# One weight decode, one token-sum step, one passage decode and two low halves moved in an attention, GLU and MLP kernel

## The chip, the cores and the metric

The kernel runs on one core of a Trainium2 chip. The time is microseconds on the device from the start of the launch to its end; the median of several runs is compared. Everything here is float32 work: each product of two float32 matrices is made of three TensorE passes over a high and a low part, high by high, high by low and low by high.

## The reference

```python
x = attn_out.transpose(0, 2, 1, 3).reshape(2304, 512)   # linear attention over 4 x 8 heads, 576 tokens
xn = x / sqrt(mean(x * x) + 1e-6) * rms_g
x = (silu(xn @ w_gate) * (xn @ w_val)) @ w_out           # 512 -> 1536 -> 512
h = x @ w2_in                                            # 512 -> 2048
out = (h * sigmoid(h)) @ w2_out                          # 2048 -> 512
```

The weights come as 64-bit floats. The kernel loads them as pairs of 32-bit words and turns them into float32 by itself.

## The kernel before

The tokens stand in five blocks: blocks 0 to 3 have 512 tokens, block 4 has 256. `xs[j]` holds a block's input as a high and a low part. The 12 GLU slices (128 columns of `w_gate` and `w_val`, 128 rows of `w_out`) and 16 MLP slices are worked through in turn, all blocks for a slice before the next. Slices 0 and 1 and slice 2 (`sweeps`) are done with plain three-pass products, 12 matmuls of 128x128 by 128x512 for a block. From slice 3 on (`groups`, nine of the GLU and eight pairs of the MLP) `quad` computes two blocks at once from sums of weights and sums of tokens, so that seven half products do the work of eight.

**Decoding weights.** A slice is loaded by a DMA on SP's queue into one of two buffers, raw0 or raw1. `w_decode` (`dec`) takes five steps on VectorE (L146 to L157) and two adds on GpSimd (L160); after them the raw buffer is free for the next load. Then ScalarE makes the high part (`hi`, with four scalings at L168 for gate and value, and L486) and VectorE the low one (`lo`, L490). `sum12` and `sum34` (GpSimd, L376) and `shi`, `slo` make the sums of weights. `WeightQueue.plan` lists these jobs for each group; an entry that is only `(0,)` does nothing. `tick` runs the next entry. In `stream` the products yield their planned TensorE time, and the driving loop at the end of the kernel runs a tick when enough of it has gone by, unless `quiet`, `calm` or `hold` is set; `quad` sets `hold` and calls `tick` at places written out by hand.

**Token sums.** `token_sums` returns a list of steps: sums and differences on VectorE (L407, L410), `tok_high` on ScalarE (L399) and `tok_low` on VectorE (L402). The loop pops one after each `wq.rest` of planned time. For the second pair of blocks `tok_high(2)` writes into `ya[1]`.

**The order at the first `quad`.** In `stream`, `order` goes through (3, f0), (4, f0), (1, slice 2), (0, slice 2), (3, slice 2), (2, slice 2), (4, slice 2). The output products (`g2_glu`, L281) of one entry are emitted inside the value product of the next (`mixed` in `g1_glu`). For blocks 1 and 0 the outputs are copied by ScalarE (L293) to stages, which GpSimd adds into DRAM with accumulating DMAs (L297, two for a block); block 1's stages are the halves of `ya[1]`. Every block's `h` is split into a high part (ScalarE, L198) and a low one (VectorE, L199) behind the gate-value product (L242). At the entry (0, slice 2), `wq.tick()` runs the first entry of the queue:

```python
(0, lambda: dec(a0, 0), lambda: load(u, bs[0], 0)),
```

that is, the decode of group 0's gate weights from raw0 and the load of its `w_out` slice into raw0. The last step of group 0's token sums issues the load of the value weights into raw1, on the same queue.

**The passage from GLU to MLP.** Group 9 (`std`) is the first MLP group. Its decodes run in the last GLU group's second `quad`, whose ticks stand after each half product. There, block 3's last outputs are added (L303), made into a high part by ScalarE (L305) and a low part by VectorE (`low`, L271). `plus` (L658) adds `e` to a product in PSUM, which frees that bank for the next product.

Of the kernel before, what the change touches and what calls it, by code (L numbers as in the profile page):

```python
# [20 lines left out]
def kernel(  # L21
# [22 lines left out]
    KC = DM // P  # L44
# [14 lines left out]
    NB, NE = len(blocks), 3  # L59
# [162 lines left out]
    def g1_glu(f, j, hs, mid):  # L222
        wq.need((1, "g", f))
        p = ps_tile("ps_g" if blocks[j] == TB * P else "ps_y", [P, blocks[j]])
        yield from proj2(wt[1, "g", f], j, p)
        s = pools["s"][0].tile([P, blocks[j]], F32, tag="s", name="s", bufs=pools["s"][1])
        nc.scalar.activation(out=s, in_=p, func=AF.Silu)
        mixed = f == sweeps[1][1][0] and blocks[j] == TB * P
        if blocks[j] == TB * P and not mixed:
            yield from mid  # L230
        wq.need((1, "v", f))
        p = ps_tile("ps_g" if blocks[j] == TB * P else "ps_y", [P, blocks[j]])
        last = proj2(wt[1, "v", f], j, p)
        if mixed:
            yield next(last)
            step = next(last)
            yield from mid
            wq.calm, wq.quiet = True, False
            yield step
        yield from last  # L240
        wq.calm = False
        nc.vector.tensor_tensor(out=s, in0=s, in1=p, op=ALU.mult)  # L242
        if mid is None:
            wait.append(lambda: hs.update({f: split_h(s, j)}))
            return
        hs[f] = split_h(s, j)
        if blocks[j] < TB * P:
            yield from mid
# [15 lines left out]
    def g2_glu(fs, j, hs, first, last, calm=False):  # L264
        wq.need(*[(1, "o", f) for f in fs])
        staged = j < NE and not last
        y = ya[j].rearrange("p (c t) -> p c t", c=KC)
        nn = 3 * len(fs)

        def low(d):  # L270
            (nc.gpsimd if 0 < j < NE else nc.vector).tensor_tensor(  # L271
                out=xs[j][:, 1, d, :], in0=y[:, d, :],
                in1=xs[j][:, 0, d, :].bitcast(F32), op=ALU.subtract,
            )

        for d in range(KC):
            ps = ps_tile("ps_y", [P, blocks[j]])
            n = 0
            for f in fs:
                for a, c in PASS:  # L280
                    nc.tensor.matmul(  # L281
                        out=ps,
                        lhsT=wt[1, "o", f][:, a, d * P:(d + 1) * P],
                        rhs=hs[f][:, c, :],
                        start=(n == 0),
                        stop=(n == nn - 1),
                    )
                    n += 1
            if staged:
                if d % 2 == 0:  # L290
                    o = stage()
                if d % 2 == 0 or calm:
                    nc.scalar.activation(out=o[:, d % 2, :], in_=ps, func=AF.Copy)  # L293
                else:
                    nc.vector.tensor_copy(out=o[:, 1, :], in_=ps)
                if d % 2:
                    nc.gpsimd.dma_start(  # L297
                        out=kept(j, d // 2), in_=o.rearrange("p t d -> p (t d)"), accum_op=ALU.add
                    )
            elif first:  # L300
                nc.scalar.activation(out=y[:, d, :], in_=ps, func=AF.Copy)
            else:
                nc.vector.tensor_tensor(out=y[:, d, :], in0=ps, in1=y[:, d, :], op=ALU.add)  # L303
            if last:
                nc.scalar.activation(out=xs[j][:, 0, d, :], in_=y[:, d, :], func=AF.Copy)  # L305
                if d:
                    low(d - 1)
                if d == KC - 1:
                    low(d)
            yield nn * blocks[j] / 2365  # L310

# [47 lines left out]
            yield 0.216 * nn  # L359

    KH = KC // 2
    tok, sums, ready, wait, owed, stages = {}, [], set(), [], [], []

    def stage():
        stages.append(stages.pop(0))
# [3 lines left out]
    std = next(u for u, g in enumerate(groups) if g[0] == 2)  # L369
# [13 lines left out]
    def token_sums(p, temp, end, early=False, eng=nc.vector):  # L383
        half = lambda j, a, h: xs[2 * p + j][:, a, KH * h:KH * (h + 1), :].bitcast(F32)
        u = {}

        def tok_high(n, x):
            if n == 1:
                tok[p, n] = [xs[2 * p + 1][:, a, :KH, :] for a in range(2)]
            elif p:  # L390
                tag = f"ya{(1, 0, 2)[n - 2]}"
                v = big.tile([P, KC * TB * P], F32R, tag=tag, name=tag)
                v = v.rearrange("p (a c t) -> p a c t", a=2, c=KH)
                tok[p, n] = [v[:, a] for a in range(2)]
            else:
                tok[p, n] = [
                    w_tile(1, 3 + 2 * (n - 2) + a).rearrange("p (c t) -> p c t", c=KH) for a in range(2)
                ]
            nc.scalar.activation(out=tok[p, n][0], in_=x, func=AF.Copy)  # L399

        def tok_low(n, x):
            nc.vector.tensor_tensor(out=tok[p, n][1], in0=x, in1=tok[p, n][0].bitcast(F32), op=ALU.subtract)  # L402
            ready.add((p, n))

        def whole(k, j, h):
            u[k] = u[1] if k == 3 and p == 0 else temp(k).rearrange("p (c t) -> p c t", c=KH)
            nc.vector.tensor_tensor(out=u[k], in0=half(j, 0, h), in1=half(j, 1, h), op=ALU.add)  # L407

        def minus(out, x, y):
            eng.tensor_tensor(out=out, in0=x, in1=y, op=ALU.subtract)  # L410

        ready.difference_update([(p, n) for n in range(1, 5)])
        return [
            lambda: whole(1, 1, 0),
            lambda: whole(0, 0, 0),
            lambda: minus(u[0], u[1], u[0]),
            lambda: whole(2, 1, 1),
            lambda: minus(u[1], u[2], u[1]),
            lambda: minus(u[2], u[2], u[0]),
            lambda: tok_high(3, u[1]),  # L420
            *([
                lambda: tok_low(3, u[1]),
                lambda: whole(3, 0, 1),
                lambda: minus(u[3], u[3], u[2]),
                lambda: tok_high(2, u[2]),
                lambda: tok_low(2, u[2]),
            ] if early else [
                lambda: (tok_low(3, u[1]), tok_high(2, u[2])),
                lambda: tok_low(2, u[2]),
                lambda: whole(3, 0, 1),  # L430
                lambda: minus(u[3], u[3], u[2]),
                lambda: None,
            ]),
            lambda: tok_high(4, u[3]),
            lambda: (tok_low(4, u[3]), end(0)),
        ], [
            lambda: tok_high(1, u[0]),
            lambda: (tok_low(1, u[0]), end(1)),
        ]

    class WeightQueue:
# [12 lines left out]
        def load(self, u, key, n):  # L454
            if u >= len(groups):
                return
            key = self.keys(u)[0][key] if isinstance(key, int) else key
            kind, nm, f = key
            src = {"g": w_gate, "v": w_val, "o": w_out, "i": w2_in, "p": w2_out}[nm]
            self.st[key] = State()  # L460
            w_load((0, 0, key, wrows(src, f) if nm in "op" else wcols(src, f)), self.st[key], n)
# [9 lines left out]
        def plan(self, u):  # L471
# [8 lines left out]
            def dec(key, n):  # L480
                for k in range(7):
                    w_decode((0, 0, key, None), st[key], k, n)
# [14 lines left out]
            def lo(key):  # L497
                split_lo(mf(key), st[key].t)
                wt[key] = st[key].t
# [55 lines left out]
            elif std <= u < std + NSTD:  # L555
# [9 lines left out]
                    (1, lambda: lo(a1), lambda: hi(a0), lambda: dec(bs[1], 1), lambda: load(u + 1, 1, 1))  # L565
                    if u == std else (1, lambda: hi(a0)),
                    (0, lambda: lo(a0)),
                    (0, lambda: dec(bs[0], 0), lambda: load(u + 1, 0, 0)),
                    *[(0,)] * (1 + (u == std)),
                    (1, lambda: hi(bs[1])),  # L570
                    (0, lambda: lo(bs[1])),
                    (0,),
# [47 lines left out]
    wq = WeightQueue()  # L620
# [11 lines left out]
    def quad(u, ys, hs, p=0, skip=0, done=True):  # L632
# [19 lines left out]
        def silu(x, tl):  # L652
            nc.scalar.activation(out=tl, in_=x, func=AF.Silu)  # L653
            return tl
# [59 lines left out]
            wq.release(("s", u, 1))  # L714
        t12 = plus(pc)
        silu(t12, t12)

        def last_half():
            if kind == 1:
# [95 lines left out]
    def stream():  # L815
# [28 lines left out]
        for n, (j, fs) in enumerate(order):  # L844
            hs, mine = {}, n == len(order) - 1
            wq.quiet = n == 3
            if n == 3:
                wq.tick()
            for f in fs:
                yield from g1_glu(f, j, hs, None if mine else pend)  # L850
                pend = pend if mine else ()
# [19 lines left out]
        for u, (kind, fs) in enumerate(groups):  # L871
# [6 lines left out]
            if std <= u < std + NSTD:  # L878
# [3 lines left out]
                    stages[:] = [ya[3][:, n * 1024:][:, :1024] for n in range(2)] + [ya[4]]  # L882
                while wait:
                    wait.pop(0)()
                each = [(2, 2)] * 4 if first else [(2, 2), (1, 1), (0, 0), (0, 0)]
                for n, k in enumerate(each):
                    if n == 2 and not first:
# [5 lines left out]
                    j = 3 - n // 2 if first else 1 - n // 2  # L893
# [767 lines left out]
    with tc.manual_schedule():  # L1661
# [50 lines left out]
        n = 0  # L1712
# [59 lines left out]
```

## Time and profile before

| | |
|---|---|
| median of 3 runs | 944.88 us (944.24 to 945.15) |
| the profiled execution | 945.14 us, of which the span of instructions is 943.3 us |
| TensorE matmul busy | 926.8 us (98% of the span) |
| VectorE, ScalarE, GpSimd busy | 703.9, 531.0, 476.2 us (75%, 56%, 50%) |
| mean granted TensorE clock | 0.994 |

PE is TensorE's matmuls, PEld its weight loads, DVE VectorE, ACT ScalarE, POOL GpSimd, SPq the queue of the sync engine, which issues DMAs. Busy time is the time in which an instruction of that engine runs. A line number is that of the kernel before.

### The profile page before, as it was taken

To read this page: it belongs to the slowest core of one execution; us is meant where nothing else is said; L and a number is where in the kernel's file an instruction comes from. 1 tells how busy PE (TensorE), PEld (TensorE's weight loads), DVE (VectorE), ACT (ScalarE), POOL (GpSimd) and SP (SyncE) were. 2 spreads that over 40 slices of the span, in tenths; PEclk is the share of its full clock that TensorE was granted. 3 is DMA by queue.
4 is the path that set the end of the run, shared out by engine and by line. 5 is a ranking of instruction groups with operands and counts; after the bars stand their busy time and mean duration, and the time that the engine had idled before them with its cause. 6 is when DMAs were issued, how large, how long until landed. Compare 5 with 4: busy or idle time off the path is not lost.

```text
span 943.3 us, 17366 instructions
## 1 busy us (share of the span) xinstructions
PE 926.8 (98%) x6480; PEld 777.2 (82%) x6480; DVE 703.9 (75%) x1323; ACT 531.0 (56%) x1157; POOL 476.2 (50%) x495
## 2 busy tenths in 40 slices
PE   8999999997999999999999989999999999999998
PEld 6888878885888888888888878888888888888886
DVE  6998999866787877877787888877674757575633
ACT  5999977644455455455545455656545454545442
POOL 8888755105445545445454644376554545453411
PEclk9999999999999999999999999999999999999999
DMA  7645543304648648658657742546878787878677
GB/s 188 170 126 149 145 131 97 151 23 92 133 89 174 139 97 184 142 101 170 153 99 151 177 158 68 183 109 133 158 129 165 136 159 143 153 150 148 113 148 165
DMA packets 98788, 129.65 MB, mean 137 GB/s; under 512 B 29456, under 2 KB 75792, under 8 KB 98704
## 3 DMA queue, kind: packets, MB, share of 16 engines
q0 software_dynamic: 17280, 59.78, 36.4%
q1 hardware_dynamic: 81152, 68.70, 25.4%
q8 instruction: 51, 0.84, 0.4%
q14 instruction: 33, 0.27, 0.1%
q10 hardware_dynamic: 272, 0.07, 0.0%
HBM read 54.59 MB, written 69.21 MB: 131 GB/s over the span
## 4 chain that ended last, share of the span: by engine, by line
PE 91%; DMA 3%; DVE 2%; POOL 2%; ACT 1%; issue 1%; SPq 0%; DVEq 0%; POOLq 0%; ACTq 0%
PE g L626 29%; PE y L333 21%; PE y L281 13%; PE g L205 7%; PE y L205 6%; PE b L1238 3%; PE b L205 3%; PE kv L1318 2%; PE b L1422 2%; PE b L1211 2%; PE b L1638 2%; POOL m L160 1%; DMA out_dram<-ya 1%; PE b L1518 1%; PE b L1398 1%; DMA raw<-in_moe_w_out_dram 1%
## 5 line engine op out<-in xcount | busy, mean ns | idle before, releaser
L160 POOL TENSOR_TENSOR m<-m,raw 128x512 int32<-128x512 int32 x136 | 202.5, 1490 | 208.2 <-DVE m L157 114.1
L333 PE MATMUL y<-w,h 128*128 128x512 f32 (+1 forms) x870 | 211.9, 388 | 0.2 <-ACT h L198 0.2
L333 PEld LDWEIGHTS y<-w,h 128*128 128x128 f32 x870 | 162.0, 188 | 34.0 <-ACT h L198 0.7
L626 PE MATMUL g<-xs,w 128*128 128x512 f32 x720 | 181.7, 390 | 0.0
L626 PEld LDWEIGHTS g<-xs,w 128*128 128x128 f32 x720 | 134.2, 188 | 27.3
L281 PE MATMUL y<-h,w 128*128 128x512 f32 (+1 forms) x648 | 150.6, 370 | 5.9 <-ACT h L198 5.9
L199 DVE TENSOR_TENSOR h<-s,h 128x512 fp32r<-128x512 f32 (+1 forms) x117 | 88.0, 764 | 89.2 <-ACT h L198 89.1
L281 PEld LDWEIGHTS y<-h,w 128*128 128x128 f32 x648 | 115.5, 191 | 28.2 <-ACT h L198 6.3
L358 POOL DMA_DIRECT2D out_dram<-ya x64 | 59.0, 987 | 117.1 <-DVE ya L352 49.4
L198 ACT ACTIVATE h<-s 128x512 fp32r<-128x512 f32 (+1 forms) x117 | 69.0, 594 | 37.5 <-DVE s L242 15.1
L350 ACT ACTIVATE ya<-y 128x512 f32<-128x512 f32 x82 | 48.9, 596 | 71.3 <-PE y L333 67.3
L297 POOL DMA_DIRECT2D out_dram<-w x52 | 46.0, 889 | 71.5 <-ACT w L293 67.0
L205 PE MATMUL g<-xs,w 128*128 128x512 f32 x336 | 80.3, 390 | 0.0
L1287 ACT ACTIVATE e<-b,nb 128x128 f32<-128x128 f32 x272 | 76.1, 425 | 7.4 <-issue 4.0
L352 DVE COPY ya<-y 128x512 f32<-128x512 f32 x52 | 35.8, 688 | 59.3 <-PE y L333 59.3
L638 ACT ACTIVATE g<-g 128x512 f32<-128x512 f32 x60 | 34.9, 581 | 70.2 <-PE g L626 69.6
L205 PEld LDWEIGHTS g<-xs,w 128*128 128x128 f32 x336 | 62.7, 188 | 12.8
L626 PE MATMUL g<-w,w 128*128 128x512 f32 x270 | 69.7, 394 | 2.7 <-DVE s L658 2.7
L490 DVE TENSOR_TENSOR w<-m,w 128x512 fp32r<-128x512 f32 x74 | 70.3, 950 | 0.2 <-ACT w L486 0.2
L653 ACT ACTIVATE s<-s 128x512 f32<-128x512 f32 x42 | 26.6, 633 | 76.5 <-DVE s L658 76.5
L626 PE MATMUL g<-ya,w 128*128 128x512 f32 x270 | 68.5, 389 | 0.0
L205 PEld LDWEIGHTS y<-xs,w 128*128 128x128 f32 x480 | 61.1, 190 | 2.1
(142 smaller groups left out, 1593.5 us busy)
## 6 DMA issues: line engine op xcount, KB each, us to landing
out_dram<-ya POOLq DMA_DIRECT2D x54, 512.0 KB, 6.9
out_dram<-w POOLq DMA_DIRECT2D x54, 512.0 KB, 7.3
raw<-in_moe_w_out_dram SPq DMA_DIRECT2D x28, 512.0 KB, 4.7
raw<-in_moe_w_in_dram SPq DMA_DIRECT2D x16, 512.0 KB, 4.6
out_dram<-ya SPq DMA_DIRECT2D x14, 512.0 KB, 4.0
raw<-in_moe_w_gate_dram SPq DMA_DIRECT2D x12, 512.0 KB, 4.1
raw<-in_moe_w_val_dram SPq DMA_DIRECT2D x12, 512.0 KB, 4.8
qT<-e SPq DMA_DIRECT2D x72, 64.0 KB, 2.3
```

Of the source, the lines that this page charges most:

```text
L160: tt(out=mi, in0=mi, in1=(low if step == 5 else high).bitcast(I32), op=ALU.add)
L198: nc.scalar.activation(out=ht[:, 0, :], in_=s, func=AF.Copy)
L199: nc.vector.tensor_tensor(out=ht[:, 1, :], in0=s, in1=ht[:, 0, :].bitcast(F32), op=ALU.subtract)
L205: nc.tensor.matmul(out=ps, lhsT=w[:, a, cc * P:(cc + 1) * P], rhs=xs[j][:, c, cc, :], start=(n == 0), stop=(n == 3 * KC - 1),)
L281: nc.tensor.matmul(out=ps, lhsT=wt[1, "o", f][:, a, d * P:(d + 1) * P], rhs=hs[f][:, c, :], start=(n == 0), stop=(n == nn - 1),)
L297: nc.gpsimd.dma_start(out=kept(j, d // 2), in_=o.rearrange("p t d -> p (t d)"), accum_op=ALU.add)
L333: nc.tensor.matmul(out=ps, lhsT=hs[f][:, a, t * P:(t + 1) * P], rhs=wt[2, "p", f][:, c, d0:d1], start=(n == 0), stop=(n == nn - 1),)
L350: nc.scalar.activation(out=o[:, t % 2, :], in_=ps, func=AF.Copy)
L358: nc.gpsimd.dma_start(out=rows, in_=o[p0:p1], accum_op=ALU.add)
L490: eng.tensor_tensor(out=v[:, 1, :], in0=x, in1=v[:, 0, :].bitcast(F32), op=ALU.subtract)
L626: nc.tensor.matmul(out=ps, lhsT=w[:, a, (c0 + c) * P:(c0 + c + 1) * P], rhs=x(b, c), start=(start and n == 0), stop=(n == 3 * KH - 1), ski ...
L1287: nc.scalar.activation(out=st.e[r][:, :, h, :] if blocks4 else st.e[r][:, h, :], in_=src.rearrange("p (a f) -> p a f", a=4) if blocks4 els ...
```

## The change

Five edits. In `g1_glu`, a tick is run for block 1 after the outputs of the entry before it and ahead of the second half of its value product; the tick at the start of the next entry goes. In `token_sums`, the list that is used early (the second pair of blocks, at the first `quad`) has an empty step ahead of `tok_high(2, ...)`. In `plan`, for group `std`, an empty entry is moved from behind the decode of `bs[0]` to ahead of it. In `g2_glu`, for block 3's last outputs, the low halves of the last two chunks are put into a list `lows`; `quad` empties it behind the add and Silu that make `t12`.

```diff
--- before.py
+++ after.py
@@ -235,6 +235,8 @@
             yield next(last)
             step = next(last)
             yield from mid
+            if j == 1:
+                wq.tick()
             wq.calm, wq.quiet = True, False
             yield step
         yield from last
@@ -303,9 +305,13 @@
                 nc.vector.tensor_tensor(out=y[:, d, :], in0=ps, in1=y[:, d, :], op=ALU.add)
             if last:
                 nc.scalar.activation(out=xs[j][:, 0, d, :], in_=y[:, d, :], func=AF.Copy)
-                if d:
+                if j == NE and d >= KC - 2:
+                    lows.append(lambda d=d: low(d))
+                    if d < KC - 1:
+                        low(d - 1)
+                elif d:
                     low(d - 1)
-                if d == KC - 1:
+                if j != NE and d == KC - 1:
                     low(d)
             yield nn * blocks[j] / 2365
 
@@ -359,7 +365,7 @@
             yield 0.216 * nn
 
     KH = KC // 2
-    tok, sums, ready, wait, owed, stages = {}, [], set(), [], [], []
+    tok, sums, ready, wait, owed, lows, stages = {}, [], set(), [], [], [], []
 
     def stage():
         stages.append(stages.pop(0))
@@ -422,6 +428,7 @@
                 lambda: tok_low(3, u[1]),
                 lambda: whole(3, 0, 1),
                 lambda: minus(u[3], u[3], u[2]),
+                lambda: None,
                 lambda: tok_high(2, u[2]),
                 lambda: tok_low(2, u[2]),
             ] if early else [
@@ -565,8 +572,9 @@
                     (1, lambda: lo(a1), lambda: hi(a0), lambda: dec(bs[1], 1), lambda: load(u + 1, 1, 1))
                     if u == std else (1, lambda: hi(a0)),
                     (0, lambda: lo(a0)),
+                    *[(0,)] * (u == std),
                     (0, lambda: dec(bs[0], 0), lambda: load(u + 1, 0, 0)),
-                    *[(0,)] * (1 + (u == std)),
+                    (0,),
                     (1, lambda: hi(bs[1])),
                     (0, lambda: lo(bs[1])),
                     (0,),
@@ -714,6 +722,8 @@
             wq.release(("s", u, 1))
         t12 = plus(pc)
         silu(t12, t12)
+        while lows:
+            lows.pop(0)()
 
         def last_half():
             if kind == 1:
@@ -844,8 +854,6 @@
         for n, (j, fs) in enumerate(order):
             hs, mine = {}, n == len(order) - 1
             wq.quiet = n == 3
-            if n == 3:
-                wq.tick()
             for f in fs:
                 yield from g1_glu(f, j, hs, None if mine else pend)
                 pend = pend if mine else ()
@@ -882,6 +890,7 @@
                     stages[:] = [ya[3][:, n * 1024:][:, :1024] for n in range(2)] + [ya[4]]
                 while wait:
                     wait.pop(0)()
+                assert not lows
                 each = [(2, 2)] * 4 if first else [(2, 2), (1, 1), (0, 0), (0, 0)]
                 for n, k in enumerate(each):
                     if n == 2 and not first:
```

## Rows read from the trace of the kernel before

**Rows 1.** The page's part 1: busy us (share of the span) xinstructions.
```profile
PE 926.8 (98%) x6480; PEld 777.2 (82%) x6480; DVE 703.9 (75%) x1323; ACT 531.0 (56%) x1157; POOL 476.2 (50%) x495
```

**Rows 2.** Waits of PE, 180 to 560 us: total, times, longest us.
```profile
PE y L281 <- ACT h L198: 5.9, 1, 5.9
PE g L626 <- DVE s L658: 2.7, 1, 2.7
```

**Rows 3.** Stretches: length, busy us of each engine, granted clock, DMA share, GB/s.
```profile
134.70:140.00 5.30, 4.13 (x48) 3.46 (x47) 4.82 (x17) 5.30 (x17) 2.61 (x4) 1.00 0.67 176
234.96:240.46 5.50, 5.50 (x13) 4.11 (x14) 4.33 (x6) 4.12 (x8) 2.41 (x3) 0.54 0.94 201
546.65:552.50 5.85, 5.85 (x30) 5.37 (x31) 4.32 (x7) 2.25 (x4) 0.49 (x1) 0.71 1.03 399
```

**Rows 4.** Timeline, 199 to 223 us: start, us, engine, line, out<-in, [idle before <-releaser].
```profile
199.02 0.39 SPq L136 DMA_DIRECT2D raw<-in_moe_w_gate_dram  x1
...
205.15 1.22 DVE L407 TENSOR_TENSOR ya<-xs 128x1024 f32<-128x1024 f32 x1
...
210.14 0.69 DVE L199 TENSOR_TENSOR h<-s,h 128x512 fp32r<-128x512 f32 x1 [0.70 <-ACT h L198]
...
212.56 2.88 PE L281 MATMUL y<-h,w 128*128 128x512 f32 x12
212.59 5.62 POOL L160 TENSOR_TENSOR m<-m,raw 128x512 int32<-128x512 int32 x2 [37.00 <-DVE m L157]
...
216.25 0.59 ACT L293 ACTIVATE ya<-y 128x512 f32<-128x512 f32 x1
...
218.16 2.01 POOL L297 DMA_DIRECT2D out_dram<-ya  x2
218.24 0.34 SPq L134 DMA_DIRECT2D raw<-in_moe_w_out_dram  x1
...
218.67 15.86 SPq L136 DMA_DIRECT2D raw<-in_moe_w_val_dram  x2
...
220.72 2.88 PE L281 MATMUL y<-h,w 128*128 128x512 f32 x12
221.33 1.22 DVE L410 TENSOR_TENSOR w<-w,ya 128x1024 f32<-128x1024 f32 x1
```

**Rows 5.** Timeline, 228 to 249 us.
```profile
228.76 0.43 DVE L146 TENSOR_SCALAR m<-raw 128x512 uint32<-128x512 uint32 x1 [6.20 <-DMA raw<-in_moe_w_val_dram]
...
230.06 1.06 ACT L399 ACTIVATE ya<-ya 128x1024 fp32r<-128x1024 f32 x1 [7.85 <-DMA out_dram<-ya]
...
231.02 1.07 ACT L293 ACTIVATE w<-y 128x512 f32<-128x512 f32 x2
...
234.96 5.50 PE L281 MATMUL y<-h,w 128*128 128x512 f32 x12 [5.92 <-ACT h L198]
...
245.19 0.69 DVE L490 TENSOR_TENSOR w<-ws,w 128x512 fp32r<-128x512 f32 x1
...
247.04 1.52 PE L626 MATMUL g<-xs,w 128*128 128x512 f32 x6
```

**Rows 6.** DMA issues: KB each, us to landing; then the landing of `out_dram`, 205 to 260 us.
```profile
raw<-in_moe_w_val_dram SPq DMA_DIRECT2D x12, 512.0 KB, 4.8
...
DMA to landing us min/median/max: 7.0/8.3/11.0
```

**Rows 7.** Timeline, 539 to 550 us.
```profile
539.33 1.80 DVE L490 TENSOR_TENSOR w<-m,w 128x512 fp32r<-128x512 f32 x1
...
542.23 0.43 DVE L146 TENSOR_SCALAR m<-raw 128x512 uint32<-128x512 uint32 x1 [1.11 <-DMA raw<-in_moe_w_out_dram]
...
543.92 1.28 DVE L303 TENSOR_TENSOR ya<-y,ya 128x512 f32<-128x512 f32 x2
...
545.91 0.68 DVE L658 TENSOR_TENSOR s<-g,e 128x512 f32<-128x512 f32 x1
...
546.65 2.49 PE L626 MATMUL g<-w,w 128*128 128x512 f32 x6 [2.67 <-DVE s L658]
```

## The prediction

> **What bounds the kernel now.** I read the shares of busy time first: TensorE is busy 98% of the span, VectorE, the next, 75% [rows 1]. So time can only be won where TensorE idles or runs slowly, and the list of waits says where. After the attention stage two waits are worth naming: 5.9 us, once, for ScalarE's high half of a GLU block, and 2.7 us, once, for VectorE's add of `e` at L658 [rows 2]. Then I asked for the granted clock in the stretch behind each. It was 0.54 in the 5.50 us behind the first and 0.71 in the 5.85 us behind the second; in a stretch that holds an idle of about 1.2 us (5.30 - 4.13) it stayed at 1.00 [rows 3]. So each of the two long waits is paid for twice, once as idle time and once as matmuls on the lower of the two clock levels, 1.2 instead of 2.4 GHz.
>
> The price of the first: 5.92 us idle [rows 5], and 12 output products of 5.50 us [rows 5] where the same 12 took 2.88 us a block earlier [rows 4], 2.62 more. Together 8.54. Of the second: 2.67 idle [rows 7], and 5.85 x (1 - 0.71) = 1.70 [rows 3]. Together 4.37. Both gone would be 12.91 us.
>
> **Why TensorE waits the first time.** The timeline has two causes that end within 1.3 us of each other. VectorE stands at `dec` of the value weights until 228.76, because their load has not landed. That load was issued at 218.67 (the row merges it with a later one), right behind the `w_out` load at 218.24, which could go only when GpSimd's two adds of the gate's decode (212.59 + 5.62) had let go of the raw buffer [rows 4, 5]. And ScalarE stands until 230.06 at `tok_high(2)`, which writes into `ya[1]`, the stage that block 1's accumulating DMAs still read; GpSimd issued those only at 218.16, behind the same two adds [rows 4, 5]. Behind that wait on ScalarE's queue are two of block 0's output copies (1.07 us), the gate's scaling and high half, the last copy, and then the high half of block 3 that TensorE needs [rows 5]. Mending one cause alone would leave the other, so the two edits belong together.
>
> **The tick inside block 1's value product.** It issues the same five VectorE steps, two GpSimd adds and one `w_out` load as before; nothing is added. On VectorE they come behind the sum that ends at 205.15 + 1.22 = 206.37 [rows 4]. Five steps take 543.92 - 542.23 = 1.69 us [rows 7], so the adds may start at 208.1, not 212.59. They read the gate weights, loaded at 199.02 [rows 4]; with the value loads' median of 4.8 us [rows 6] that landed by 204, with the slowest load here (228.76 - 218.67 = 10.1) at 209.1. I take the median, so no wait. At their full 5.62 us the adds end at 213.7: `w_out` goes then, the value load 0.43 later, at 214.1. It lands at 218.9 (median) to 224.2 (10.1 again). VectorE doesn't come to that decode before 221.33 + 1.22 = 222.55 [rows 4]. So it starts at 222.6 to 224.2, where it was 228.76. Past block 1's outputs, GpSimd's accumulating DMAs no longer stand behind the adds: the second is issued when its last copy is done, at 216.25 + 0.59 = 216.84 [rows 4]. Landing here took 7.0 to 11.0 us [rows 6], so 223.8 to 227.8. I take 224.4, near the low end, because the two weight loads that shared the DMA engines with the 11.0 are by then mostly done.
>
> The Trainium skill ("DMA: Bandwidth & Descriptors", section "Anatomy of one DMA") fits such a transfer as 2.0 us plus its bytes at 436 KB per us, which would make 3.2 us for 512 KB. No landing of these accumulating transfers came near that [rows 6], so the measurement decides; by the page's figure ScalarE would not wait at all, and the sum would be about 0.7 us lower.
>
> **The empty step.** Sum steps are popped once per 1.5 us of planned TensorE time, and an output yields 0.65. By that count `tok_high(2)` moves from behind block 0's first output copy to behind its third, and the token steps after it each move one place, into block 2's products. It costs no instruction. The third copy ends at about 220.72 + 3/4 x 2.88 + 0.6 = 223.5 [rows 4], so ScalarE loses little by coming there later. From the start of `tok_high(2)` to TensorE's restart took 234.96 - 230.06 = 4.90; less the 1.07 of two copies that are now in front, 3.8 [rows 5]. TensorE arrives at 234.96 - 5.92 = 229.04. So the DMA may land as late as 225.2 without a wait. At 224.4 the high half is ready at 228.2, 0.8 ahead.
>
> **What is late next.** VectorE then has a queue. From the restart to the end of the first sum's low half, which TensorE needs for its first sum product, took 245.19 + 0.69 - 234.96 = 10.9 us [rows 5]; one of the token steps (1.22 us each, [rows 4]) now comes after the restart point, so up to 12.1. Starting at 228.2 it ends at 239.1 to 240.3. TensorE comes to that product at 247.04 - 8.54 = 238.50 [rows 5]. That is a new wait of 0.6 to 1.8 us, or none if VectorE, which has fewer idle moments now, is quicker. I take 0.7, near the end that was measured, and no clock loss, since an idle of 1.2 left the clock alone [rows 3].
>
> **The decode in the passage.** In the GLU's last group VectorE is at the head of a line: done with a low half at 539.33 + 1.80 = 541.13, it waits 1.11 us for the load of a `w_out` slice, decodes it until 543.92, does two output adds and one low half (1.99) and only then, at 545.91, the add at L658 that frees TensorE [rows 7]. The empty entry moved ahead makes the tick before that add do nothing; the decode comes at the tick after it. So 541.13 + 1.99 + 0.68 = 543.80 for the end of the add. TensorE's idle began at 546.65 - 2.67 = 543.98 [rows 7]. The wait goes, with 0.2 us to spare; I leave 0.1 for it, and 0.5 as the bound. The decode's load was the thing awaited and has landed by 542.23, so at 543.8 it costs its 1.69 and no wait. What issues with it, the next group's load into that raw buffer, goes some 1.5 us later; its decode stands behind a barrier in the job list until that group, which hides this.
>
> **Block 3's last two lows.** They would otherwise stand with the late decode in front of the next add at L658. They are moved behind that add and beside ScalarE's Silu. No engine does more. By the durations above block 3's last low ends near 543.8 + 1.69 + two adds (1.28) + a low (0.7) + the add (0.68) + two lows (1.4) = 549.6. TensorE needs it for the second half of block 3's first MLP product: 543.98 and six products (1.4), a small GLU block of 24 half-width ones (2.8), six products (1.4) and six outputs (1.4), 551.0. Cost 0; without that cover up to 1.4.
>
> **The sum.** 945.14 - 8.54 - 4.37 + 0.7 + 0.1 = 933.03 in the profiled execution; the median of the runs, 944.88, lies 0.26 below that execution, so 932.8.
>
> **The rivals.**
> - *The first wait comes back in part.* If the accumulating DMA lands at 227.8, the high half is ready at 231.6, 2.6 late, and the clock falls as behind the second wait: 2.6 + 1.7 - about 4.3 more, or 937. It decides from 225.2 on. For it: 11.0 was measured here [rows 6]. Against: then it ran beside two loads. Chance 0.12.
> - *The second wait stays.* If the two adds are held up by something that the decode hid, only the first is gained: about 937.1. The margin is 0.2 us, but half a microsecond of lateness costs only itself. Chance 0.06.
> - *GpSimd's adds hold up VectorE.* The gate's adds now run where block 1's split (L199, 210.14) stands. If it had to wait for both, to 213.7, it would end at 214.4, while TensorE's second product there needs it at 212.56 + 0.2 [rows 4]: 1.6 us idle, to 3.3 with the clock: 934.4 to 936.1. A rule of the Trainium skill ("SBUF — State Buffer", "Who interferes with whom") says just that: a VectorE operation with two SBUF inputs and a GpSimd one that reads SBUF exclude each other for a whole instruction. The trace agrees in part: an L490 took 1.80 us here [rows 7] where another took 0.69 [rows 5]. But an instruction is one add, not both, and one add from 208.1 is over by about 210.9. Chance 0.03.
> - *Slower: the lead at the first sum product is lost for good.* That product came 247.04 - 245.88 = 1.2 us after its weights [rows 5]. If the 8.5 us pause was what let VectorE keep ahead, TensorE waits at that place in each of the nine GLU groups. From 12.9/9 = 1.4 us a group there is no gain; at the 4.37 of the second wait it is 945 + 9 x 4.37 - 12.9, 971. Against: VectorE is busy 75% [rows 1], so a deficit is made up within a group. Chance 0.03.
> - *Nothing happens,* because the order on the engines comes out as before: 944.9. Chance 0.01.
>
> **How the numbers follow.** The forecast, both waits gone and up to 2 us of new ones, has the rest, 0.75; its own range is 931.7 to 934.4. The 8 in 10 range is 931.6 (no new wait, less the spread of the runs) to 937.2, which takes in the first two rivals. A change under 0.2%, about 1.9 us, can't be told from none here. Faster: all but the last two, a little off for what I haven't seen: 0.94; same 0.02; slower 0.04.
>
> **What would show it.** Right: the gate's first decode step on VectorE near 206, GpSimd's adds near 208, both loads on SP's queue before 215, the value decode without a wait before 225, and no wait over 1 us in TensorE's list behind 180 us except perhaps one at the first sum product; near 530 an add at L658 ahead of the decode, and the clock at 1.00 in both places. Wrong: a wait of ScalarE's L399 for `out_dram<-ya` beyond 225.2, or waits that return group by group.

## The result, and the profile after

| | before | after |
|---|---|---|
| median (lowest to highest), 6 runs each | 945.2 us (944.24 to 945.67) | 936.19 us (933.84 to 938.1) |
| the profiled execution, its span | 945.14 us, 943.3 us | 937.75 us, 936.0 us |

The ratio is 0.9905, with a 95% interval of 0.9889 to 0.9922: faster by about 1%. The forecast was 932.8 (range 931.6 to 937.2), so the time lies inside the range, 3.4 us above the forecast and 1.8 above the likeliest case's own range.

TensorE's busy time fell by 1.8 us [rows 1], the rest of what went was idle; those of VectorE, ScalarE and GpSimd moved by less than 1.5 us (the page's part 1):

```profile
PE 925.0 (99%) x6480; PEld 775.0 (83%) x6480; DVE 705.2 (75%) x1323; ACT 529.8 (57%) x1157; POOL 474.8 (51%) x495
```

TensorE's waits of the whole launch (total, times, longest): the two of [rows 2] are gone, and three small ones stand behind the attention stage.

```profile
PE y L283 <- ACT h L198: 0.7, 1, 0.7
PE y L283 <- DVE ya L305: 0.5, 1, 0.5
PE y L283 <- DVE h L199: 0.2, 1, 0.2
```

The granted clock is back too. Windows where the two slow stretches of [rows 3] were: block 3's outputs, block 2's (0.89 us of idle in it), and the passage, all at 1.00, the higher of the two levels, 2.4 GHz.

```profile
230.99:234.14 3.15, 3.03 (x13) 2.18 (x12) 2.62 (x4) 1.52 (x3) 0.38 (x1) 1.00 1.03 234
239.00:242.50 3.50, 2.61 (x11) 1.61 (x10) 2.71 (x6) 1.98 (x5) 0.30 (x1) 1.00 0.00 0
536.00:545.00 9.00, 9.00 (x52) 7.80 (x51) 8.90 (x15) 2.50 (x4) 5.46 (x4) 1.00 0.79 273
```

**A ledger by stage.** To put every microsecond in its place I took four marks on TensorE's timeline that every version has: A, the first plain product behind attention; B, the first product of the first `quad` on `ya`; C, the last GLU group's last product on `xs`; D, the first MLP output product (timeline of after):

```profile
180.18 11.06 PE L205 MATMUL g<-xs,w 128*128 128x512 f32 x48
...
257.57 1.52 PE L634 MATMUL g<-ya,w 128*128 128x512 f32 x6
...
538.74 1.52 PE L634 MATMUL g<-xs,w 128*128 128x512 f32 x6
...
568.42 5.60 PE L339 MATMUL y<-w,h 128*128 128x512 f32 x24
```

| us | A (attention) | B-A (first pause) | C-B | D-C (passage) | end-D | end-A |
|---|---|---|---|---|---|---|
| before | 178.07 | 83.37 | 281.02 | 33.34 | 367.50 | 765.23 |
| forecast | 178.07 | 75.53 | 281.02 | 29.07 | 367.50 | 753.12 |
| after | 180.18 | 77.39 | 281.17 | 29.68 | 367.58 | 755.82 |

The row "forecast" is before's with the prediction's prices taken off. The first stretch gave 5.98 us, the passage 3.66, all else behind A cost 0.23: 9.41 behind attention. Attention itself, whose instructions are the same, ended 2.11 us later in this execution, which is why its span fell by 7.3 only. In all 14 profiles of this study A lies between 175.99 and 180.26, so versions are compared by end-A, and the medians of the runs beside it. Below, a time "in before's time" has those 2.11 taken off.

Now the timeline behind block 1's value product (start, us, engine, line, [idle <- what ended it]), to be held against [rows 4] and [rows 5]:

```profile
208.40 0.42 DVE L146 TENSOR_SCALAR m<-raw 128x512 uint32<-128x512 uint32 x1
...
210.24 2.70 POOL L160 TENSOR_TENSOR m<-m,raw 128x512 int32<-128x512 int32 x2 [32.54 <-DVE m L157]
...
212.25 1.24 DVE L199 TENSOR_TENSOR h<-s,h 128x512 fp32r<-128x512 f32 x1 [0.70 <-ACT h L198]
...
212.96 0.34 SPq L134 DMA_DIRECT2D raw<-in_moe_w_out_dram  x1
...
213.41 1.21 DVE L408 TENSOR_TENSOR xs<-raw,xs 128x1024 fp32r<-128x1024 f32 x1
...
214.65 14.84 SPq L136 DMA_DIRECT2D raw<-in_moe_w_val_dram  x2
...
219.25 0.87 POOL L299 DMA_DIRECT2D out_dram<-ya  x1 [1.00 <-ACT ya L295]
...
224.55 0.42 DVE L146 TENSOR_SCALAR m<-raw 128x512 uint32<-128x512 uint32 x1
...
226.83 1.06 ACT L405 ACTIVATE ya<-ya 128x1024 fp32r<-128x1024 f32 x1 [1.15 <-DMA out_dram<-ya]
...
230.99 3.31 PE L283 MATMUL y<-h,w 128*128 128x512 f32 x12
```

In before's time the gate's decode starts at 206.3 and GpSimd's adds at 208.1, as was forecast. The adds took 2.70, less than half of the 5.62 that they took in the kernel before. The value decode has no wait in its row, ScalarE waits 1.15 us where it waited 7.85 [rows 5], and TensorE goes into block 3's outputs with no wait.

### The profile page after: what moved, and what is told of

Read it like the earlier page. It is cut to its first block, busy times and chain, and to the rows that moved or that the text cites. A ratio compares the mean times of both kernels' runs of the same rounds, so it can differ in the third digit from the quotient of the medians.

```text
span 936.0 us, 17366 instructions
## 1 busy us (share of the span) xinstructions
PE 925.0 (99%) x6480; PEld 775.0 (83%) x6480; DVE 705.2 (75%) x1323; ACT 529.8 (57%) x1157; POOL 474.8 (51%) x495
## 4 chain that ended last, share of the span: by engine, by line
PE 78%; DVE 3%; ACT 2%; issue 1%; DMA 1%; POOL 0%; DVEq 0%; ACTq 0%; POOLq 0%
PE g L634 29%; PE y L339 21%; PE y L283 12%; PE g L205 6%; PE y L205 5%; PE b L1647 2%; PE b L205 1%; DMA out_dram<-ya 1%; PE b L1431 1%; DVE ya L305 1%; DVE xs L273 0%; DVE w L497 0%; PE b L1527 0%; ACT h L198 0%; ACT ya L405 0%
## 5 line engine op out<-in xcount | busy, mean ns | idle before, releaser
L160 POOL TENSOR_TENSOR m<-m,raw 128x512 int32<-128x512 int32 x136 | 200.0, 1472 | 197.4 <-DVE m L157 107.0
L199 DVE TENSOR_TENSOR h<-s,h 128x512 fp32r<-128x512 f32 (+1 forms) x117 | 88.1, 764 | 89.6 <-ACT h L198 89.5
```

Source lines behind the costliest of these rows:

```text
L160: tt(out=mi, in0=mi, in1=(low if step == 5 else high).bitcast(I32), op=ALU.add)
L199: nc.vector.tensor_tensor(out=ht[:, 1, :], in0=s, in1=ht[:, 0, :].bitcast(F32), op=ALU.subtract)
```

## The experiments

The forecast rests on two edits that belong together for the first pause, a decode and two lows for the second, and a wait of 0.7 us for VectorE's queue. The rivals: one of the two edits does it alone; a part costs something; the new wait is somewhere else. Every kernel here computes the whole reference. Each median stands beside that of the kernel before on the same chip.

**The tick alone** (`tick_only`), on the kernel before:

```diff
             yield from mid
+            if j == 1:
+                wq.tick()
...
-            if n == 3:
-                wq.tick()
```

> Of the five edits only the moved tick in block 1's value product. Theory 1 (the tick by itself frees the value load and GpSimd's accumulating DMAs, and both land about 3.5 us sooner): ScalarE waits for the DMA only to about 47 us behind the stage's first product (52 before), VectorE not at all, and of TensorE's 5.9 us wait about 1 stays; 938 to 940. Rival (two causes, each enough: without the empty step ScalarE still stands until the DMA lands about as late as before): TensorE still waits 4 us or more, 943 to 945.

**The empty step alone** (`empty_only`), on the kernel before:

```diff
                 lambda: minus(u[3], u[3], u[2]),
+                lambda: None,
                 lambda: tok_high(2, u[2]),
```

> Only the empty step in the early token sums. Theory 1: the value load still lands 10 us after its issue, VectorE stands until then, and ScalarE waits for the DMA as long as before, but with two output copies (1.07 us) in front of it; TensorE's wait falls from 5.9 to about 4.9, 943.5 to 944.5. Rival (the DMA wait on ScalarE is the one that counts): the wait falls to 3 us or less, 940 to 942.

**Both, without the passage** (`first_pair`): the two diffs above together.

> The tick and the empty step, nothing at the passage. Theory 1 (what was lost against the forecast is lost right behind the first wait, on VectorE's queue): TensorE's long wait goes, 2.5 us come back as short waits in the first quad; 6.0 us gained, 939 to 940, and the 2.7 us wait at the passage is there unchanged. Rival (the loss is a longer attention stage in this program): the quads run 7.8 us sooner against the stage's first product, and the attention stage is 2 us longer than before in the profile and the times are spread over 4 us.

**The passage alone** (`passage`), on the kernel before: the moved empty entry and the two late lows, the whole change's other edits.

```diff
                     (0, lambda: lo(a0)),
+                    *[(0,)] * (u == std),
                     (0, lambda: dec(bs[0], 0), lambda: load(u + 1, 0, 0)),
-                    *[(0,)] * (1 + (u == std)),
+                    (0,),
...
+        while lows:
+            lows.pop(0)()
```

> The empty entry moved ahead of the passage's decode and the two lows, nothing at the first quad. Theory 1: the 2.7 us wait and its slow clock go (4.4 us), and 0.5 to 0.8 come back as a wait for VectorE's output adds some 20 us later; 941 to 942. Rival (nothing comes back here): 940.5 to 941. The first wait of 5.9 us is there unchanged. If the attention stage of a changed program is longer or scattered, this shows it too.

| | median (lowest to highest), us | ratio [95%] | B-A | D-C | end-A |
|---|---|---|---|---|---|
| tick_only | 939.16 (936.04 to 941.27) | 0.9919 [0.99, 0.9939] | 76.19 | 33.18 | 758.04 |
| empty_only | 945.47 | 0.9994 [0.9984, 1.0003] | 82.60 | 34.66 | 766.08 |
| first_pair | 939.32 | 0.9927 [0.9913, 0.9941] | 76.71 | 33.47 | 758.90 |
| passage | 941.67 | 0.9949 [0.9936, 0.9963] | 83.98 | 29.70 | 762.29 |

The tick alone takes 7.18 us of the first pause, which was priced at 8.54. The empty step alone makes no difference that the times of the runs show. In its profile the first stretch is 0.77 us shorter and the passage 1.32 longer; the granted clock behind the passage's wait was 0.54 there (546.56 to 553.00) and 0.73 in before (546.65 to 553.00), so nearly the same wait can cost more in one execution than in another. The two halves of the change add up: behind attention first_pair gains 6.3 and passage 2.9 us, the whole 9.4. The timelines show why. With the tick alone ScalarE waits only 1.63 us for the DMA, TensorE 0.20 and 0.39 (timeline of tick_only):

```profile
226.03 1.07 ACT L401 ACTIVATE ya<-ya 128x1024 fp32r<-128x1024 f32 x1 [1.63 <-DMA out_dram<-ya]
...
231.68 2.80 PE L283 MATMUL y<-h,w 128*128 128x512 f32 x11 [0.20 <-DVE h L199]
...
237.64 1.68 PE L205 MATMUL y<-xs,w 128*128 128x256 f32 x12 [0.39 <-DVE ya L305]
```

With the empty step alone all three waits of the kernel before are still there, shorter by 1.1 to 1.8 us (timeline of empty_only), and the slow outputs behind them, 5.16 us:

```profile
227.31 0.43 DVE L146 TENSOR_SCALAR m<-raw 128x512 uint32<-128x512 uint32 x1 [4.39 <-DMA raw<-in_moe_w_val_dram]
...
230.26 1.06 ACT L399 ACTIVATE ya<-ya 128x1024 fp32r<-128x1024 f32 x1 [6.35 <-DMA out_dram<-ya]
...
234.21 5.16 PE L281 MATMUL y<-h,w 128*128 128x512 f32 x12 [4.81 <-ACT h L198]
```

**Which of the two causes ended last** (`load_split`), on the kernel before. The decode stays where it was, but the value load no longer stands behind the `w_out` load on SP's queue:

```diff
-                    (0, lambda: dec(a0, 0), lambda: load(u, bs[0], 0)),
-                    (0,),
+                    (0, lambda: dec(a0, 0)),
+                    (0, lambda: load(u, bs[0], 0)),
                     (0,),
```

> The kernel before with one move of its own: the w_out load that stood behind the gate's decode is issued one queue entry later, behind the value load; the decode and GpSimd's adds stay where they were. Theory 1 (the wait for the accumulating DMA ended last, the one for the value load just ahead of it): VectorE's wait of 6.2 us goes or falls under 2, ScalarE's stays within 2 us of its 7.9, and TensorE still waits 3 to 5.5 us; 1 to 4 us under before. Rival (the value load is what counts, the DMA only came late because of it): TensorE waits 1 us or less; 6 to 8 under before.

944.16 us beside 945.05 (ratio 0.9993, 0.9985 to 1.0002), slightly less than the 1 to 4 us expected; B-A 82.36, end-A 764.30. The load goes 5 us earlier and its decode starts with no wait in its row, yet ScalarE still waits 6.33 us for the accumulating DMA, and TensorE 4.39 (timeline of load_split):

```profile
213.70 0.39 SPq L136 DMA_DIRECT2D raw<-in_moe_w_val_dram  x1
...
222.51 0.42 DVE L146 TENSOR_SCALAR m<-raw 128x512 uint32<-128x512 uint32 x1
...
228.56 1.06 ACT L399 ACTIVATE ya<-ya 128x1024 fp32r<-128x1024 f32 x1 [6.33 <-DMA out_dram<-ya]
...
233.47 5.79 PE L281 MATMUL y<-h,w 128*128 128x512 f32 x12 [4.39 <-ACT h L198]
```

So the accumulating DMA is the cause that ended last, and VectorE's wait for the load lay in its shadow.

**The whole change without the empty step** (`no_empty`): the `lambda: None,` is taken out again.

> The change without the empty step in the token sums. Theory 1 (the step moves a token step of 1.2 us on VectorE into the queue behind the first wait and wins nothing back): from the stage's first product to the first quad's double product 73.5 us, where the whole change has 74.7; 9.5 to 10.5 us under before. Rival (the step is needed, as the prediction has it): ScalarE's wait for the accumulating DMA reaches TensorE, 1 us or more idle at block 3's outputs, 8 us or less under before.

**The whole change without the late lows** (`no_lows`): each low directly behind its high half, as before.

> The change without its last edit: block 3's last two low halves stand where they stood, ahead of the second add of e. Theory 1 (they stand beside work that TensorE does not wait for): as the whole change, 9 us under the kernel before, within 1 us. Rival (with the decode moved behind the first add, two lows more in front of the second add make the blocks behind late): TensorE waits 1 us or more between the last add of e and the second MLP block, only 7 to 8 us under before.

**The whole change with the last token steps later** (`late_sums`): the rest of the second pair's list (`later23`) is handed to the driving loop behind the entry (4, slice 2) instead of behind (3, slice 2).

```diff
                 del stages[:2]
-                sums.extend(later23)
             out = g2_glu(fs, j, hs, j >= NE and fs is f0, False, fs is f0 or j < NE)
...
         wq.free += [(1, 0), (1, 1)]
+        sums.extend(later23)
         wq.tick()
```

> The whole change, and the last two token steps of the second pair of blocks (one of 1.05 us on ScalarE, one of 1.2 to 1.7 on VectorE) put off until the first quad, which does not read them. Theory 1 (VectorE's queue is what makes block 2's split late in the whole change): block 2's gate-value product comes 1.5 us sooner, the waits of 0.66 and 0.23 us at its outputs go, and about 1 to 1.5 us are gained on the whole change; 10 to 11 under before. Rival (the split waits for something else, or the steps come back as a wait in the second quad): no gain, within 0.5 us of the whole change.

**The same without the empty step** (`no_empty_late`):

> Both: without the empty step, and the last two token steps put off. Theory 1: both lighten the same queue, so they add up only until the waits there are gone; 10.5 to 11.5 us under before, the first quad's double product at 73.0 us or less behind the stage's first product. Rival (they are independent): 11.5 or more. If the queue is not the cause, no better than the whole change, 9.

**A second empty step** on the whole change (`double_empty`), to price one:

```diff
                 lambda: None,
+                lambda: None,
                 lambda: tok_high(2, u[2]),
```

> The whole change with two empty steps in place of one. Theory 1 (what counts is which token steps stand on VectorE's queue ahead of block 2's split; by the count of planned time the second empty step moves the last token step behind it): the first quad comes as early as with the last token steps put off, 75.3 us behind the stage's first product by the mark that is at 77.4 in the whole change's profile, 10 us or more under before. Rival (each empty step costs what the first one did, 0.8 us): 77.5 or later, 8 to 9 under before.

**The whole change once more** (`after_2`, nothing edited) and **no_empty_late once more** (`best_2`), side by side:

> The whole change again, beside the next one on the same chip. Theory 1 (its times are scattered by the attention stage, which ends at 176.4 to 180.3 us in ten profiles of the same code, and by short waits in the first quad): 9 to 10 us under before, and behind the attention stage 755 to 756 us. Rival (a property of this program): its attention stage ends near 180 again.

> Without the empty step and with the last two token steps put off, again, beside the whole change. Theory 1: behind the attention stage 753.3 us, 2 to 3 us less than the whole change. Rival (the gain over the whole change was the attention stage's): within 1 us of it.

| | median (lowest to highest), us | ratio [95%] | A | B-A | D-C | end-A |
|---|---|---|---|---|---|---|
| after | 936.19 (933.84 to 938.1) | 0.9905 [0.9889, 0.9922] | 180.18 | 77.39 | 29.68 | 755.82 |
| after_2 | 934.7 (933.08 to 936.62) | 0.9891 [0.9877, 0.9905] | 180.14 | 76.32 | 29.69 | 754.66 |
| no_lows | 936.1 | 0.9905 [0.9889, 0.9921] | 178.80 | 76.13 | 31.35 | 756.20 |
| no_empty | 932.67 | 0.9869 [0.9854, 0.9884] | 176.42 | 75.68 | 29.67 | 753.98 |
| late_sums | 933.52 | 0.9876 [0.9853, 0.99] | 178.79 | 75.29 | 29.69 | 753.71 |
| no_empty_late | 932.79 | 0.987 [0.9855, 0.9884] | 177.97 | 74.94 | 29.69 | 753.33 |
| best_2 | 933.77 (932.84 to 934.77) | 0.9881 [0.9867, 0.9894] | 177.29 | 75.93 | 29.68 | 754.31 |
| double_empty | 932.66 (930.92 to 933.22) | 0.9871 [0.9856, 0.9886] | 175.99 | 74.87 | 29.70 | 753.21 |

With no empty step the kernel is not slower than with one. With two of them its median is 2.0 us under that of after_2 on the same chip (the intervals overlap a little) and its end-A 1.45 under. So a step has no fixed price, neither way. What differs is how many of VectorE's `tok_low` steps (L408 in the kernel after) stand between block 3's split and block 2's add at L244: three in after, after_2, first_pair and no_lows (B-A 76.13 to 77.39), two in no_empty, late_sums and double_empty (74.87 to 75.68), one in no_empty_late and best_2 (74.94 and 75.93). tick_only has two as well and 76.19, with waits in other places. In the whole change the step at 236.99 (1.71 us, L408) and two output adds come ahead of that add, block 2's split is late, and TensorE waits 0.66 and 0.23 us (timeline of after):

```profile
236.99 1.71 DVE L408 TENSOR_TENSOR xs<-w,xs 128x1024 fp32r<-128x1024 f32 x1
...
238.62 1.28 DVE L305 TENSOR_TENSOR ya<-y,ya 128x512 f32<-128x512 f32 x2
239.82 0.67 DVE L244 TENSOR_TENSOR s<-s,g 128x512 f32<-128x512 f32 x1
...
241.20 0.50 PE L283 MATMUL y<-h,w 128*128 128x512 f32 x1 [0.66 <-ACT h L198]
241.93 0.73 PE L283 MATMUL y<-h,w 128*128 128x512 f32 x2 [0.23 <-DVE h L199]
```

With two empty steps that token step comes behind the split, and neither wait is there (timeline of double_empty):

```profile
232.14 0.68 DVE L244 TENSOR_TENSOR s<-s,g 128x512 f32<-128x512 f32 x1
...
233.52 0.69 DVE L199 TENSOR_TENSOR h<-s,h 128x512 fp32r<-128x512 f32 x1 [0.70 <-ACT h L198]
234.13 1.22 DVE L408 TENSOR_TENSOR xs<-w,xs 128x1024 fp32r<-128x1024 f32 x1
```

There B-A is 74.87, the 74.83 of a pause that goes without any new wait. That its end-A, 753.21, comes so near the forecast's 753.12 is luck: its first stretch is 0.66 us shorter than forecast, its passage 0.63 longer.

Without the late lows the passage takes 1.67 us longer. VectorE does both last lows ahead of the add (L273, then L662), and TensorE waits twice (timeline of no_lows):

```profile
541.55 1.80 DVE L273 TENSOR_TENSOR xs<-ya,xs 128x512 fp32r<-128x512 f32 x2
543.28 0.68 DVE L662 TENSOR_TENSOR s<-g,e 128x512 f32<-128x512 f32 x1
...
546.67 0.97 PE L283 MATMUL y<-h,w 128*128 128x512 f32 x3 [0.69 <-ACT both L764]
548.05 0.96 PE L283 MATMUL y<-h,w 128*128 128x512 f32 x3 [0.42 <-DVE both L761]
```

Its median equals the whole change's, as expected, though the two waits add up to the 1 us or more that its rival named. So those 1.67 us are shown by the ledger alone, not by the times of the runs.

no_empty, late_sums and no_empty_late came 11.8 to 12.6 us under before on the same chip, more than the 9.5 to 11.5 expected; behind attention they gain 11.3 to 11.9 on before. no_empty_late is no faster than no_empty, so the two edits don't add up. best_2 missed its expectation: its end-A is 0.35 us under that of after_2, not 2 to 3, as its rival had it, and what else its profile gains is A, 2.85. In it ScalarE waits 2.40 us for the accumulating DMA and TensorE 0.47 and 0.22 at block 3's outputs, so without the empty step a late landing does reach TensorE.

## Why the prediction was right, and where it was not

**Right: both pauses, each priced as idle time and lower clock.** The two waits went, and with them the granted 0.54 and 0.71. The first stretch with no new wait, 83.37 - 8.54 = 74.83, was reached by double_empty (74.87) and no_empty_late (74.94).

**Right: the tick.** Decode and adds came to the tenth where they were forecast, the value decode's wait went, and the accumulating DMA had landed at 226.83, in before's time 224.7, where 224.4 was forecast. The reason given for taking that near-low value, that two weight loads are mostly done by then, no run tested. Two sizes were off and cost nothing: the adds took 2.70 instead of 5.62, and the value load was held not by the `w_out` load but by the token step that issues it (213.41 + 1.21, then 214.65).

**Wrong: "Mending one cause alone would leave the other, so the two edits belong together."** The tick alone mends both, because both causes stand behind the same two GpSimd adds; the prediction's own paragraph on the tick had already moved the DMA's landing to 224.4, and only the 225.2 up to which that has no price hung on the empty step. What it could save is what tick_only's first stretch has above 74.83, 1.36 us, of which 0.20 + 0.39 are waits, and first_pair does not save it: B-A 76.71 against 76.19, end-A 758.90 against 758.04, the medians 0.16 us apart. It can matter when the DMA lands late, as best_2 shows. As load_split shows, of the two causes it is the DMA that had to be mended.

**Mis-sized: "I take 0.7" for what is late next.** The mechanism, VectorE's queue behind the first pause, was right. From block 3's split to the end of the first sum's low half it took 12.23 us, about the 12.1 that the prediction gave with one token step more; the forecast went by 10.9, the length without it. The first sum product started at 242.50, in before's time 240.39, which is 1.89 later than the 238.50 of a pause without a new wait (timeline of after):

```profile
230.76 0.69 DVE L199 TENSOR_TENSOR h<-s,h 128x512 fp32r<-128x512 f32 x1 [2.89 <-ACT h L198]
...
242.31 0.68 DVE L497 TENSOR_TENSOR w<-ws,w 128x512 fp32r<-128x512 f32 x1
...
242.50 1.75 PE L634 MATMUL g<-xs,w 128*128 128x512 f32 x6
```

The four profiles with tick and empty step (77.39, 76.71, 76.13, 76.32) have a mean of 76.64, 1.8 above 74.83: the upper end that the prediction gave. The place was for the most part another. The first sum product itself is slower by only 0.23 us (1.75, [rows 5] 1.52); ahead of it block 2's split is late (0.66 + 0.23). In after block 3's outputs took 3.31 us where 2.88 was taken [rows 4]; in after_2, first_pair and no_lows they took 2.88. In after_2 ScalarE doesn't wait for the DMA at all, and B-A is 1.07 shorter than in after. Block 4's six half-width outputs took 1.32 us (0.88 in before): the high half of their `h` stands on ScalarE's queue behind one of weights, which waited 0.94 us for a GpSimd add:

```profile
247.85 0.63 ACT L493 ACTIVATE w<-m 128x512 fp32r<-128x512 f32 x1 [0.94 <-POOL m L160]
248.39 0.40 ACT L198 ACTIVATE h<-s 128x256 fp32r<-128x256 f32 x1
...
248.85 1.32 PE L283 MATMUL y<-h,w 128*128 128x256 f32 x6
```

I had followed the token steps up to the weights that TensorE needs next on VectorE's list, and not asked of every VectorE result in between whether a step now stands ahead of it.

**The passage: right but for 0.46 us.** The add now precedes the decode, and TensorE doesn't wait. What comes back is one wait further on, for block 4's output add (timeline of after); it is in every version with the edit (0.44 to 0.51), and not in those without it.

```profile
539.31 0.68 DVE L666 TENSOR_TENSOR s<-g,e 128x512 f32<-128x512 f32 x1
539.91 0.42 DVE L146 TENSOR_SCALAR m<-raw 128x512 uint32<-128x512 uint32 x1
540.10 1.59 PE L634 MATMUL g<-w,w 128*128 128x512 f32 x6
...
565.21 0.62 PE L283 MATMUL y<-h,w 128*128 128x256 f32 x3 [0.46 <-DVE ya L305]
```

**The late lows: cost 0, right.** Taking them back costs 1.67 in the ledger, where up to 1.4 was given for the loss of the cover.

**The rivals.** The accumulating DMA landed before 225.2 (in before's time), so the first wait did not come back. The split that stands beside GpSimd's adds took 0.55 us longer (L199 1.24, [rows 4] 0.69) and cost TensorE nothing: both adds were over at 212.94, and when it began, at 212.25, more than half of their 2.70 us had gone by, so the second alone can have held it up. That agrees with the rule of the Trainium skill ("SBUF — State Buffer", "Who interferes with whom") that a VectorE instruction with two SBUF inputs contends with a GpSimd one that reads SBUF. No wait returned group by group: C-B is 281.17, before 281.02.

**The remaining difference to the forecast.** Behind attention the profile of after ends 2.70 us above it: 1.86 in the first stretch, 0.61 in the passage, 0.23 elsewhere. The rest of that execution's difference is A. Whether the change has a part in A stays open. Both profiles of the whole change end attention near 180.2, the sign that after_2's rival named, tick_only's too, but first_pair, which has the same tick, at 178.70; the instructions are the same, and no run here changed that stage. In the three profiles near 180.2 TensorE's listed waits for loads in that stage (`vat`, `x`) come to 1.9 to 2.6 us, in before to 0.2; but empty_only and no_empty_late have 2.2 and 2.1 and end it at 178.4 and 178.0, so the loads are a part at most. The forecast's range had no room for A: two of the six runs, 937.75 and 938.1, lie above its upper end, so that the median lies inside is in part luck.

**A faster version.** double_empty, no_empty and no_empty_late lie at 0.987 of the kernel before, late_sums and best_2 at 0.988, the whole change at 0.989 to 0.9905. The intervals of the first three lie below that of the whole change's first runs (0.9889 to 0.9922) and overlap with that of after_2 (0.9877 to 0.9905), so the medians alone put the gain at 0 to 0.4%. The ledger, over all pairs of these profiles, puts 0.4 to 2.6 us behind attention, nearly all in the first stretch; the rest is A. That fewer token steps ahead of block 2's split are the cause rests on the timelines of single profiles and on late_sums, which only moves the last two token steps (one of them ScalarE's): there neither wait at block 2's outputs is left.

## What to carry to other kernels

When two late things wait for the same third one, look first at what moving that third one does to both, before adding an edit for each. Price a long TensorE wait with the lower clock behind it, from the same products in another place. And when a pause goes, list every result that the busiest helper engine owes in the next blocks, in order, since a step moved by one place costs whatever now stands behind it.

## What the runs showed of the hardware that was not expected

The accumulating DMAs of this stretch, 512 KB each, took 5.3 to 11.0 us to land in the versions shown, and 5.2 to 11.2 in all 14: 7.0/8.3/11.0 (lowest, median, highest) before [rows 6], and in the same stretch of after and of double_empty:

```profile
DMA to landing us min/median/max: 5.7/7.8/8.6
```

```profile
DMA to landing us min/median/max: 5.3/7.3/8.9
```

The 3.2 us, an estimate from the fit in the Trainium skill ("DMA: Bandwidth & Descriptors", "Anatomy of one DMA"), were not seen in any of them.

Two GpSimd adds took 5.62 us in one place and 2.70 in another, with the same tiles. The time goes with the place: 2.68 to 2.71 us in all ten versions with the moved tick, 5.61 or 5.62 in the four without it. In the old place three VectorE steps with two SBUF inputs run beside them (L402 and twice L410, 1.22, 1.22 and 2.22 us), in the new one only L199 (1.24). No run here separates the cause. And the attention stage, with the same instructions in every kernel, ended anywhere in 175.99 to 180.26 us: a spread of 4.3 us, more than the 2.9 by which the run passage gained behind attention.
